# One test of a sum in place of two around the guarded slots, and the last kept slot's output moved behind it on GpSimd

## The chip, the core and the metric

The kernel runs on one core of a Trainium2 chip. Its engines are PE (TensorE, matmuls, with PEld for the loads of stationary operands), DVE (VectorE), ACT (ScalarE), POOL (GpSimd) and SP (SyncE, which here only issues transfers). Each engine has a sequencer that takes its own instructions in order and waits on semaphores; in the profile's rows an engine's name with a q behind it (POOLq, SPq) is that sequencer. The metric is the device time of one execution in microseconds (us).

## What is computed

A linear attention with random features gives `x`, and a mixture of experts is applied to each token of `x`:

```python
proj = np.einsum('bhsd,df->bhsf', x, w_phi)
proj = proj - np.max(np.abs(proj), axis=-1, keepdims=True)
phi = np.concatenate([np.exp(proj), np.exp(-proj)], axis=-1)   # for q and for k
kv = np.einsum('bhsf,bhsd->bhfd', k_p, v); z = np.sum(k_p, axis=2)
attn = einsum(q_p, kv) / (einsum(q_p, z) + 1e-6)               # -> x, (8, 576, 512)
...
logits = x @ w_gate                                            # 8 experts
fresh_e = argmax(logits); e = fresh_e if s == 0 or local_gate < 0.5 else prev_e
out[b, s] = softmax(logits)[e] * (np.maximum(x[b, s] @ w1[e], 0.0) @ w2[e])
```

There are 8 x 576 = 4608 tokens. Which expert a token goes to, and so how many tokens each expert gets, is known only on the device.

## The kernel before

The first half of the kernel computes the attention, 128 rows at a time, and the gate; each token's index and probability are scattered into a list by expert. The second half works through *slots*. A slot is one expert's weights with one, two or four groups of 128 tokens of that expert: quads (four groups), pairs (two) and singles (one), and *duals*, in which two half-filled groups of two experts share one group. A slot gathers its tokens by an indirect transfer from GpSimd (`gather_x`), transposes them, runs layer 1 (`layer1`) and layer 2 (`layer2`), scales the result by the probability into a tile `y` on DVE (line 948), and writes `y` to the rows of `out` by another indirect transfer from GpSimd (line 949). Weights arrive through SP as `wraw`, ACT casts them to a high part `whi` (line 797) and DVE forms the rest `wlo` (line 798); ACT and DVE do the same for the layer-1 result, `hh` (line 896) and `hl` (line 897).

`plan_main` (from line 662) counts, on DVE, how many slots of each kind the drawn tokens need. The lists are sized for the largest case. Ten singles are laid out and four duals; `moe` (line 988) always runs the first four singles and the first two duals, mixed among the quads and pairs, and the last of that order is a single. The six other singles and two other duals are *guarded*: each is in a branch that is entered only when the count says so, one nested in the other (`guarded`, line 982). The counts are two integers in memory, `left` (singles needed) and `halves` (half groups needed). Every engine loads `left` (line 999), compares and branches (line 984), then loads `halves` (line 1001) and branches again. With the data of this case no guarded slot is entered.

A tile that an engine writes or a transfer fills is guarded by semaphores that count. An engine that jumps over a guarded block therefore runs a short false path instead, in which it adds to its semaphores what the skipped instructions would have added. On GpSimd this is a wait for each of its eight transfer semaphores (DMASW0 to DMASW7) and then one INC_SWDGE_SEM, which adds to them. At the end every engine takes a DRAIN and meets the others at two barriers; SP first checks all the final semaphore values.

A scheduler orders the instructions of each engine by readiness and priority; on PE the order of the first half is written out by hand.

Of the kernel before, what the change touches and what calls it, by code (L numbers as in the profile page):

```python
# [6 lines left out]
F32 = mybir.dt.float32  # L7
F32R = mybir.dt.float32r
BF16 = mybir.dt.bfloat16
I32 = mybir.dt.int32  # L10
AF = mybir.ActivationFunctionType
ALU = mybir.AluOpType
# [5 lines left out]
DM, E, FF = 512, 8, 1024  # L18
# [3 lines left out]
NT = B * S  # L22
# [21 lines left out]
HALFWAY, EARLY, QUADS, PAIRS, SINGS, GUARD, DUALS, GUARD_D = 2, 3, 3, 7, 10, 6, 4, 2  # L44
# [4 lines left out]
class Kernel:  # L49
# [555 lines left out]
    def plan_early(self, bp):  # L605
# [39 lines left out]
        if bp == 1:  # L645
            yield from self.early_chores(slots, got())
        else:

            g = got()
            for x in g:  # L650
                if not self.scattering:
                    break
                yield x

            def last():
                for _ in g:
                    pass
                for s in slots:
                    self.gather_x(s)
            self.fetched_last = last  # L660

    def plan_main(self):
        dve = self.dve
        cq, size, half, mq, mp, ms, mps = (self.slotc[:, i:i + 1] for i in range(7))
        u1, u = self.units_so_far(127, 7, "m1"), self.units_so_far(63, 7, "m")
# [5 lines left out]
        ih = self.prefix(hf, "ih")  # L671
# [8 lines left out]
        for z in (0, 1):  # L680
            name = f"h{z}"
# [26 lines left out]
        i1 = self.prefix(f1, "i1")  # L708
        self.left = self.psm([1, 1], "left", I32)
        dve.tensor_copy(self.left, i1[0:1, E - 1:E])  # L710

        def mix(a, b, c, name):
            t = self.psm([NU, E], name)
            dve.tensor_scalar(t, a, mq, None, ALU.mult)
            dve.scalar_tensor_tensor(t, b, mp, t, ALU.mult, ALU.add)
            dve.scalar_tensor_tensor(t, c, ms, t, ALU.mult, ALU.add)
            return t

        incl = mix(i4, i2, i1, "im")
        cnt = mix(f4, f2, f1, "cm")  # L720

        bef = self.psm([NU, E], "bef")
# [11 lines left out]
        f = self.fetch(es, k, NU, "m", 1, rh)  # L734
        next(f)
        yield
        try:
            next(f)
        except StopIteration as r:
            tok, prob = r.value  # L740
        at = 0
# [183 lines left out]
            self.used(1)  # L925
        return [lambda: turn(2), lambda: turn(3)]

    def layer2(self, s, gi, between):
        tc, dve, pool = self.tc, self.dve, self.pool
        hh, hl = s["h"][gi]  # L930
        u0 = s["u"] + sum(s["n"][:gi])
        for k in range(s["n"][gi]):
            self.l2n = getattr(self, "l2n", 0) + 1
            p = self.psr if hasattr(self, "psr") and self.l2n % 3 else self.psm4
            t = p.tile([128, DM], F32, name="l2")
            o = slice(k * 128, k * 128 + 128)
            for f in range(8):
                c = slice((f % 2) * DM, (f % 2) * DM + DM)
                self.both(s, 4 + f // 2, t, hh[:, f, o], hl[:, f, o], c, f == 0, f == 7)
                if f in (0, 2) and between:  # L940
                    between.pop(0)()
                if f % 2 and gi == len(s["n"]) - 1 and k == s["n"][gi] - 1:
                    self.used(1)
                elif f % 2:
                    self.spare()
            y = self.mx2.tile([128, DM], F32, name="y")
            u = u0 + k
            dve.tensor_scalar_mul(y, t, s["prob"][:, u:u + 1])  # L948
            ins = pool.indirect_dma_start(  # L949
                self.A["out"], bass.IndirectOffsetOnAxis(s["tok"][:, u:u + 1], 0), y, None,  # L950
                bounds_check=NT - 1, oob_is_err=False)
            tc.declare_no_dep(ins.ins, group="outs", reason="each token is written once")
            tc.add_to_no_dep_group("outs", ins.ins)

    def slots(self, order, asides={}, final=None):
        first = order[0]
        for g in range(len(first["n"])):
            for f in self.tokens(first, g):
                f()
        self.held = len(first.get("w", ()))  # L960
        self.coming = list(order)
        for i, s in enumerate(order):
            while len(s.get("w", ())) < 8:
                self.spare()
            new = order[i + 1] if i + 1 < len(order) else None
            last = len(s["n"]) - 1
            for gi in range(last):
                self.layer1(s, gi, [])
            between = self.tokens(new, 0) if new else [lambda: None, final] if final else []
            rest = self.layer1(s, last, between)  # L970
            if i in asides:
                asides[i]()
            for f in between:
                f()
            for gi in range(last + 1):
                self.layer2(s, gi, rest)
            if new and len(new["n"]) == 2:
                for f in self.tokens(new, 1):
                    f()
            s.clear()  # L980

    def guarded(self, slots, count, i, per):
        if i < len(slots):
            with self.tc.If(count > per * i):
                self.slots([slots[i]])
                self.guarded(slots, count, i + 1, per)

    def moe(self):

        few = self.ss[:SINGS - GUARD]  # L990
        for i, x in enumerate(self.ds[:DUALS - GUARD_D]):
            few.insert(3 * i, x)
        rest = self.qs + self.ps_
        order = []
        per = len(rest) / len(few)
        for i, x in enumerate(few):
            order += rest[round(i * per):round((i + 1) * per)] + [x]
        self.slots(order)
        left = self.nc.values_load(self.left, min_val=0, max_val=63)  # L999
        self.guarded(self.ss, left, SINGS - GUARD, 1)  # L1000
        halves = self.nc.values_load(self.halves, min_val=0, max_val=63)
        self.guarded(self.ds, halves, DUALS - GUARD_D, 2)


def body(tc, A):
# [78 lines left out]
```

## Time and profile before

| | us |
|---|---|
| median of 3 runs (832.83 to 834.94) | 834.59 |
| the profiled execution | 827.76 |
| its span, first to last instruction | 825.9 |
| mean granted clock of PE in it | 0.982 of full |

The profiled execution's time stands 1.9 us above its span. A row of a group reads: line, engine, operation, output <- input, count, and durations or busy time. A row of the timeline reads: start, duration, engine, line, operation, tiles, and in brackets how long the engine had been idle before it and what ended that. The busy digits of the page, here PE and the DMA share in 40 equal slices of the span, show that PE is loaded nearly throughout and that the last slice and a half is empty:

```profile
PE   6999999999978899889999999999999999999980
DMA  6554556855898633473942775833966689867100
```

### The profile page before, as it was taken

How to read it: one execution, taken by the hardware profiler on the slowest of the kernel's cores; microseconds unless marked ns; L12 is line 12 of the kernel's file. 1: busy time of each engine (PE TensorE's matmuls, PEld its weight loads, DVE VectorE, ACT ScalarE, POOL GpSimd, SP SyncE). 2: the span in 40 equal slices, each digit the busy share in tenths (PEclk: the TensorE clock that was granted, in tenths of full speed). 3: DMA queues.
4: the chain of work that ended last, by engine and by line, in shares of the span. 5: the costliest groups of instructions: out<-in, count | busy, mean ns of one | idle time of the engine just before them, and what ended most of it. 6: DMA issues, size and time to landing. Idle time of an engine off the chain costs nothing. (4 is left out here: it accounts for less than half of the span.)

```text
span 825.9 us, 23190 instructions
## 1 busy us (share of the span) xinstructions
PE 772.5 (94%) x9674; PEld 681.2 (82%) x9674; DVE 519.9 (63%) x945; ACT 400.9 (49%) x708; POOL 138.9 (17%) x154
## 2 busy tenths in 40 slices
PE   6999999999978899889999999999999999999980
PEld 5899988888877888878888997698998996789970
DVE  5677898689778886748744224544856715776510
ACT  4666666566656565432632123533745515664410
POOL 0000002200230231242511202102222212011110
PEclk9999999999999999999999999999999999999995
DMA  6554556855898633473942775833966689867100
GB/s 194 140 134 129 145 130 117 129 137 132 151 216 226 177 77 85 107 182 106 388 166 90 264 281 205 270 115 111 356 220 211 219 312 409 303 238 238 53 28 15
DMA packets 74994, 148.71 MB, mean 180 GB/s; under 512 B 9044, under 2 KB 48610, under 8 KB 74864
## 3 DMA queue, kind: packets, MB, share of 16 engines
q1 hardware_dynamic: 67424, 127.33, 51.5%
q0 software_dynamic: 7392, 19.49, 7.0%
q8 instruction: 80, 1.31, 0.8%
q10 hardware_dynamic: 64, 0.30, 0.1%
q14 instruction: 34, 0.28, 0.1%
HBM read 128.18 MB, written 19.73 MB: 179 GB/s over the span
## 5 line engine op out<-in xcount | busy, mean ns | idle before, releaser
L797 ACT CAST whi<-wraw 128x1024 fp32r<-128x1024 f32 x136 | 142.2, 1048 | 154.5 <-PE l L865 67.1
L798 DVE TENSOR_TENSOR wlo<-wraw,whi 128x1024 fp32r<-128x1024 f32 x136 | 166.1, 1223 | 79.1 <-ACT whi L797 77.3
L863 PE MATMUL l<-xhi,whi 128*128 128x256 f32 x512 | 147.9, 289 | 3.5 <-DVE hl L897 2.8
L864 PE MATMUL l<-xlo,whi 128*128 128x256 f32 x512 | 145.5, 284 | 0.3 <-DVE xlo L859 0.3
L865 PE MATMUL l<-xhi,wlo 128*128 128x256 f32 x512 | 145.1, 283 | 0.0
L188 DVE TENSOR_REDUCE m<-pj 128x8 f32<-128x1024 f32 x72 | 87.8, 1219 | 46.4 <-PE pj L185 46.1
L863 PE MATMUL l<-whi,hh 128*128 128x512 f32 x288 | 114.2, 396 | 0.3 <-DVE y L948 0.3
L208 ACT ACTIVATE qp<-qt 128x512 f32<-128x512 f32 x144 | 84.6, 604 | 60.5 <-PE qt L205 58.2
L865 PE MATMUL l<-whi,hl 128*128 128x512 f32 x288 | 113.1, 393 | 0.0
L864 PE MATMUL l<-wlo,hh 128*128 128x512 f32 x288 | 112.8, 392 | 0.0
L194 ACT ACTIVATE kp<-sb 128x512 f32<-128x512 f32 x144 | 82.9, 623 | 53.2 <-DVE sb L190 44.3
L863 PEld LDWEIGHTS l<-xhi,whi 128*128 128x128 f32 x512 | 99.0, 194 | 6.2 <-DVE hl L897 3.4
L864 PEld LDWEIGHTS l<-xlo,whi 128*128 128x128 f32 x512 | 98.9, 193 | 1.0 <-DVE xlo L859 0.5
L865 PEld LDWEIGHTS l<-xhi,wlo 128*128 128x128 f32 x512 | 98.9, 193 | 0.1
L185 PE MATMUL pj<-first,kq 64*128 64x128 f32 x1152 | 87.2, 291 | 6.8 <-DMA kq<-in_kqT 6.4
L286 PE MATMUL nm<-kvs,qp 128*64 128x74 f32 x2304 | 87.0, 228 | 4.1 <-issue 3.1
L190 DVE TENSOR_TENSOR sb<-pj,m 128x1024 f32<-128x1024 f32 x72 | 88.1, 1223 | 3.6
L286 PEld LDWEIGHTS nm<-kvs,qp 128*64 128x64 f32 x2304 | 79.4, 136 | 5.1 <-issue 3.4
L185 PEld LDWEIGHTS pj<-first,kq 64*128 64x128 f32 x1152 | 72.7, 193 | 12.8 <-issue 5.9
L949 POOL DMA_INDIRECT out<-y,p_tokm x32 | 40.2, 1256 | 254.9 <-DVE y L948 254.3
L227 PE MATMUL kvp<-v,kp 128*64 128x65 f32 x2048 | 76.5, 224 | 0.3 <-issue 0.2
L896 ACT ACTIVATE hh<-l 128x512 fp32r<-128x512 f32 x64 | 38.1, 595 | 71.6 <-PE l L865 71.6
(229 smaller groups left out, 1037.6 us busy)
## 6 DMA issues: line engine op xcount, KB each, us to landing
wraw<-in_w1h SPq DMA_DIRECT2D x68, 512.0 KB, 5.9
wraw<-in_w2h SPq DMA_DIRECT2D x68, 512.0 KB, 6.3
kq<-in_kqT SPq DMA_DIRECT2D x47, 384.0 KB, 3.8
v<-in_va SPq DMA_DIRECT2D x48, 195.0 KB, 3.3
xs<-xo SPq DMA_DIRECT2D x48, 128.0 KB, 4.3
whi<-in_w1h SPq DMA_DIRECT2D x8, 512.0 KB, 4.2
wlo<-in_w1h SPq DMA_DIRECT2D x8, 512.0 KB
whi<-in_w2h SPq DMA_DIRECT2D x8, 512.0 KB, 7.2
```

What stands on the lines that cost most here:

```text
L185: self.last_pe = self.pe.matmul(t[:, h, i % 2, j, :], kq[r, j, s], self.w2[r], start=True, stop=True)
L188: dve.tensor_reduce(m, f, AX.X, ALU.max, apply_absolute_value=True)
L190: self.last_dve = dve.tensor_sub(sb.rearrange("p h c j f -> p (h c j) f"), f, m.unsqueeze(2).broadcast_to([128, 8, 128]))
L194: self.last_act = act.activation(kp[:, :, :, sg, :].rearrange("p c h f -> p h c f"), sb[:, :, :, 0], AF.Exp, scale=1.0 - 2 * sg)
L208: self.act.activation(qp[:, sg], t, AF.Exp, scale=1.0 - 2 * sg)
L227: self.pe.matmul(self.kvp[r, sg, h], self.ch[i]["kp"][:, h, sg, r], self.v(i, b)[:, h], start=first and n < 2, stop=last and n >= 6)
L286: self.pe.matmul(e["t"][r, c - c0, h, :], self.ch[i]["qp"][:, sg, h, q0 + r.start:q0 + r.stop], kvs[:, sg, h, :], start=sg == 0, stop=sg == 1)
L797: self.act.copy(hi, raw)
L798: self.dve.tensor_sub(lo, raw, hi.bitcast(F32))
L863: mm(o, ah, bh, start=first, stop=False)
L864: mm(o, ah, bl, start=False, stop=False)
L865: self.last_pe = mm(o, al, bh, start=False, stop=last)
```

## The change

`plan_main` gets three more operations on single numbers. They form `over` = max(left - 4, 0) + max(halves - 4, 0), which is above zero exactly when one of the two guarded lists would be entered. `moe` tests `over` once; the loads of `left` and `halves` and both nests of branches move inside that test. The last kept slot's output transfer isn't issued in `layer2` any more but handed back in a list (`held`) and issued after the test, from a tile `yl` of its own with one buffer.

```diff
+        over = self.psm([1, 2], "over")
+        dve.tensor_scalar(over[:, 0:1], i1[0:1, E - 1:E], float(GUARD - SINGS), 0.0, ALU.add, ALU.max)
+        dve.tensor_scalar(over[:, 1:2], ih[0:1, E - 1:E], float(2 * (GUARD_D - DUALS)), 0.0, ALU.add, ALU.max)
+        self.over = self.psm([1, 1], "overi", I32)
+        dve.tensor_add(self.over, over[:, 0:1], over[:, 1:2])
...
-    def layer2(self, s, gi, between):
+    def layer2(self, s, gi, between, held=None):
...
-            y = self.mx2.tile([128, DM], F32, name="y")
+            y = self.mx2.tile([128, DM], F32, name="yl", bufs=1) if held is not None else self.mx2.tile([128, DM], F32, name="y")
             u = u0 + k
             dve.tensor_scalar_mul(y, t, s["prob"][:, u:u + 1])
-            ins = pool.indirect_dma_start(
-                self.A["out"], bass.IndirectOffsetOnAxis(s["tok"][:, u:u + 1], 0), y, None,
-                bounds_check=NT - 1, oob_is_err=False)
-            tc.declare_no_dep(ins.ins, group="outs", reason="each token is written once")
-            tc.add_to_no_dep_group("outs", ins.ins)
+
+            def put(y=y, at=s["tok"][:, u:u + 1]):
+                ins = pool.indirect_dma_start(self.A["out"], bass.IndirectOffsetOnAxis(at, 0), y, None,
+                                              bounds_check=NT - 1, oob_is_err=False)
+                tc.declare_no_dep(ins.ins, group="outs", reason="each token is written once")
+                tc.add_to_no_dep_group("outs", ins.ins)
+            if held is None:
+                put()
+            else:
+                held.append(put)
...
-                self.layer2(s, gi, rest)
+                self.layer2(s, gi, rest, None if new else held)
...
-        self.slots(order)
-        left = self.nc.values_load(self.left, min_val=0, max_val=63)
-        self.guarded(self.ss, left, SINGS - GUARD, 1)
-        halves = self.nc.values_load(self.halves, min_val=0, max_val=63)
-        self.guarded(self.ds, halves, DUALS - GUARD_D, 2)
+
+        held = []
+        self.slots(order, held=held)
+        over = self.nc.values_load(self.over, min_val=0, max_val=63)
+        with self.tc.If(over > 0):
+            left = self.nc.values_load(self.left, min_val=0, max_val=63)
+            self.guarded(self.ss, left, SINGS - GUARD, 1)
+            halves = self.nc.values_load(self.halves, min_val=0, max_val=63)
+            self.guarded(self.ds, halves, DUALS - GUARD_D, 2)
+        for f in held:
+            f()
```

What this makes of the queues is seen in the built programs. The rows below show an instruction's line, name, tiles and the semaphores that it waits for. On GpSimd, at the end of the kept slots, before (the first row is the output before the last, the second the last one):

```order
L949 DMA out<-y,p_tokm 4608x512 [waits DMASW3_49,DVE_49]
L949 DMA out<-y,p_tokm 4608x512 [waits DMASW4_49,DVE_49]
L999 TENSOR_LOAD p_left [waits DVE_49]
L984 COMPARE_AND_BRANCH
L825 DMA xg<-xs,p_tokm 128x512 [waits DMASW5_49,PE_49]
```

And now, in the changed program's line numbers, up to the first guarded gather:

```order
L957 DMA out<-y,p_tokm 4608x512 [waits DMASW3_49,DVE_49]
L1012 TENSOR_LOAD p_overi [waits DVE_49]
L1013 COMPARE_AND_BRANCH
L1014 TENSOR_LOAD p_left
L995 COMPARE_AND_BRANCH
L831 DMA xg<-xs,p_tokm 128x512 [waits DMASW4_49,PE_49]
```

The test now follows the output before the last directly; the last output has gone from this place. It stands behind the false path of the test, near the end of GpSimd's program (ISA is here INC_SWDGE_SEM at line 1013, and the clearing of semaphores at line 1097):

```order
L995 ISA [waits DMASW6_49,DMASW7_49,DMASW5_49,DMASW4_49]
L995 UNCONDITIONAL_BRANCH
L1013 UNCONDITIONAL_BRANCH
L1013 ISA [waits Pool_sequencer_49,DMASW4_49,DMASW5_49,DMASW3_49,DMASW6_49,DMASW2_49,DMASW7_49,DMASW1_49,DMASW0_49]
L1013 UNCONDITIONAL_BRANCH
L957 DMA out<-yl,p_tokm 4608x512 [waits DMASW4_49,DVE_49]
L1097 UNCONDITIONAL_BRANCH
```

Before, two such false paths stood behind the last output, one for each test.

The scheduler also moves a few instructions at the start of the second half, around 385 to 422 us of the profile. On DVE, where the planning ends and the first slot's layer 1 begins, before:

```order
L562 TENSOR_SCALAR p_rim<-p_rowm 36x1
L948 TENSOR_SCALAR y<-l_6672,p_probe 128x512
L897 SCALAR_TENSOR_TENSOR hl<-l_6704,hh 128x512
L798 TENSOR_TENSOR wlo<-wraw,whi 128x1024 x2
L897 SCALAR_TENSOR_TENSOR hl<-l_6731,hh 128x512
```

And now:

```order
L562 TENSOR_SCALAR p_rim<-p_rowm 36x1
L954 TENSOR_SCALAR y<-l_6677,p_probe 128x512
L804 TENSOR_TENSOR wlo<-wraw,whi 128x1024
L903 SCALAR_TENSOR_TENSOR hl<-l_6709,hh 128x512
L804 TENSOR_TENSOR wlo<-wraw,whi 128x1024
L903 SCALAR_TENSOR_TENSOR hl<-l_6736,hh 128x512
```

The first tile's `hl` has moved behind one weight difference `wlo`; on ACT its `hh` has moved behind the cast of that weight in the same way. Some 25 us later on DVE, before:

```order
L798 TENSOR_TENSOR wlo<-wraw,whi 128x1024 [waits DMAHW3_49,Activation_49]
L948 TENSOR_SCALAR y<-l_6849,p_probf 128x512 [waits DMASW2_49,PE_49]
L798 TENSOR_TENSOR wlo<-wraw,whi 128x1024 [waits DMAHW4_49,Activation_49]
L859 TENSOR_TENSOR xlo<-tr,xhi 128x4x128 [waits Activation_49] x2
L798 TENSOR_TENSOR wlo<-wraw,whi 128x1024 [waits DMAHW0_49]
```

And now:

```order
L804 TENSOR_TENSOR wlo<-wraw,whi 128x1024 [waits DMAHW3_49,Activation_49]
L804 TENSOR_TENSOR wlo<-wraw,whi 128x1024 [waits DMAHW4_49,Activation_49]
L954 TENSOR_SCALAR y<-l_6854,p_probf 128x512 [waits DMASW2_49,PE_49]
L865 TENSOR_TENSOR xlo<-tr,xhi 128x4x128 [waits Activation_49] x2
L804 TENSOR_TENSOR wlo<-wraw,whi 128x1024 [waits DMAHW0_49]
```

That slot's `y` has moved behind one more `wlo`, and on GpSimd one output of that stretch has changed places with a gather. On SP the load of `halves` is gone from this stretch, and the load of `left` has become one of `over`. From there to the last slot the order on each engine is as before.

More of the change, by code (lines that the diff above doesn't have):

```diff
@@ L945, in layer2, with slots @@
                     self.spare()
-            y = self.mx2.tile([128, DM], F32, name="y")
+            y = self.mx2.tile([128, DM], F32, name="yl", bufs=1) if held is not None else self.mx2.tile([128, DM], F32, name="y")
             u = u0 + k
             dve.tensor_scalar_mul(y, t, s["prob"][:, u:u + 1])
-            ins = pool.indirect_dma_start(
-                self.A["out"], bass.IndirectOffsetOnAxis(s["tok"][:, u:u + 1], 0), y, None,
-                bounds_check=NT - 1, oob_is_err=False)
-            tc.declare_no_dep(ins.ins, group="outs", reason="each token is written once")
-            tc.add_to_no_dep_group("outs", ins.ins)
-    def slots(self, order, asides={}, final=None):
+            def put(y=y, at=s["tok"][:, u:u + 1]):
[7 more added lines that the diff above has]
+                held.append(put)
+    def slots(self, order, asides={}, final=None, held=None):
         first = order[0]
```

## The prediction

> **What bounds the kernel now.** I read the page first, then the stretches of the last 26 us, then the sequencer instructions of single lines there, and last the stretch around 380 to 427 us, where the order of work changes.
>
> ```profile
> span 825.9 us, 23190 instructions
> PE 772.5 (94%) x9674; PEld 681.2 (82%) x9674; DVE 519.9 (63%) x945; ACT 400.9 (49%) x708; POOL 138.9 (17%) x154
> POOL out L949 0%; POOLq L999 0%
> 600.00:803.00 203.00, 202.97 (x1306) 175.20 (x1304) 116.05 (x131) 94.83 (x133) 32.69 (x25) 1.00 0.63 226
> 800.00:804.00 4.00, 2.97 (x13) 2.06 (x11) 1.11 (x2) 0.00 (x0) 0.00 (x0) 1.00 0.03 6
> 804.00:806.00 2.00, 0.00 (x0) 0.00 (x0) 0.00 (x0) 0.00 (x0) 0.98 (x1) 0.93 0.28 90
> ```
>
> The columns of a stretch are start and end, length, busy time of PE, PEld, DVE, ACT and POOL, granted clock, DMA share and GB/s. PE is the bound up to 803 us (202.97 of 203.00). Then nothing that counts as busy happens but one POOL instruction, and the span goes on to 825.9. The chain that ended last is no help: its two entries, both 0%, stop at that instruction. The tail is made of sequencer work that no busy share shows, so I read it line by line.
>
> ```profile
> 803.00 0.75 DVE L948 TENSOR_SCALAR y<-l,p_probm 128x512 f32<-128x512 f32 x1 [2.64 <-PE l L865]
> L949 POOL DMA_INDIRECT out<-y,p_tokm x1: 983/983/983, 804.0 to 804.0; - x1
> DMA to landing us min/median/max: 5.3/5.3/5.3
> L999 POOLq TENSOR_LOAD <-p_left x1: 502/502/502, 803.8 to 803.8; - x1
> L984 POOLq EVENT_SEMAPHORE  x6: 17/43/43, 809.3 to 812.8; - x6
> L984 POOLq INC_SWDGE_SEM  x2: 2511/2520/2528, 809.7 to 812.9; - x2
> L1080 POOLq DRAIN  x3: 46/107/9617, 815.5 to 825.6; - x3
> L1080 SPq EVENT_SEMAPHORE  x14: 17/28/28, 812.1 to 825.9; - x14
> ```
>
> Each row gives count, shortest/median/longest in ns, and the first and last start. They add up to one chain on GpSimd. The last `y` is ready at 803.75; its output is issued from 804.03 to 805.02 and lands at 804.0 + 5.3 = 809.3. The branch on `left` is not taken into the guarded slots, and the path around them first waits for every GpSimd queue, the output just issued included: its first semaphore row starts at 809.3, the landing. Then one INC_SWDGE_SEM of 2.5 us (it credits the DMAs that the skipped slots would have counted), the load of `halves`, a second one from 812.9 to 815.4, and the DRAIN from 815.46 for 9.62 us to 825.08. Closing barriers take the remaining 825.9 - 825.1 = 0.8. So **the tail after the issue is 20.9 us: 4.3 to the landing, 6.1 of credits and tests, 9.6 of DRAIN, 0.8 of barriers.**
>
> **The change, part by part.**
>
> *The output behind the test.* The order shows the test of `over` on GpSimd straight behind the output before the last, and the last output (`yl`) behind the false path of that test. The credit now waits for the output before the last.
>
> ```profile
> L949 POOL DMA_INDIRECT out<-y,p_tokm x1: 983/983/983, 791.9 to 791.9; - x1
> DMA to landing us min/median/max: 2.7/6.2/8.5
> L984 POOLq COMPARE_BRANCH  x2: 45/50/54, 804.4 to 812.6; - x2
> ```
>
> It is issued at 791.9 and lands between 2.7 and 8.5 us later, at 794.6 to 800.4. Load and branch (0.5 + 0.05) lie inside that. Semaphores take 809.7 - 809.3 = 0.4, the credit 2.5: done at 797.5 to 803.3. `yl` is ready at 803.75, so even the longest landing leaves 0.4 us. Cover: PE's last slot. If it were gone, what is late is the output, us for us. The landing of 5.3 and one credit of 2.5 with its checks thus leave the path, and the second credit, its load and checks exist no more.
>
> *What is late next.* Behind `yl` stands only the branch to the end and DRAIN. With the issue over at 805.02, DRAIN starts there instead of at 815.46: **10.44 us earlier**, if it still takes 9.6. Does it? That is the unknown that matters.
>
> ```profile
> L1074 POOLq DRAIN  x1: 188/188/188, 0.3 to 0.3; - x1
> L1074 POOLq INC_SWDGE_SEM  x1: 31/31/31, 0.1 to 0.1; - x1
> lst<-pr,ri POOLq DMA_INDIRECT x36, 7.4
> xg<-xs,p_tokm POOLq DMA_INDIRECT x32, 6.7
> out<-y,p_tokm POOLq DMA_INDIRECT x32, 6.2
> ```
>
> At the start, with no GpSimd DMA behind it, DRAIN takes 0.19 us and INC_SWDGE_SEM 0.03. At the end, with these 100 and 17 smaller ones behind, 9.62 and 2.5, and the two DRAINs that follow take 0.11 and 0.05. Nothing was in flight from 809.3 on, so the long one was not waiting for data. That reads as work per earlier DMA, some 9617/117 = 82 ns each (my estimate), done once. The number of DMAs is unchanged, so I take 9.6; bounds are 0.1 (the next DRAIN) and 9.6 counted from the landing at 809.3. The walk outlasts the landing, so that one is hidden.
>
> The Trainium skill ("VectorE: DVE Perf Modes", section "The DRAIN you can't avoid") says that the closing DRAINs on all five engines are boilerplate of a constant 12 ns or so. The trace disagrees for GpSimd (9617 ns); by that sentence the long one would be a wait for something else, and the sum would come out as in the rival of the short DRAIN below.
>
> *One test in place of two, other engines.*
>
> ```profile
> L984 PEldq COMPARE_BRANCH  x2: 3847/4312/4776, 801.0 to 805.6; - x2
> L1080 PEldq DRAIN  x2: 8/8/8, 810.5 to 825.4; - x2
> ```
>
> PE loses one taken branch of 4 to 5 us and reaches its end near 806 instead of 810.5; SP's fourteen checks go from the landing on, 0.7 us of them. Both finish before 815, so both are worth nothing.
>
> *Three tiny DVE operations and a moved order, at 383 to 422 us.*
>
> ```profile
> 387.36 0.14 DVE L710 CAST p_left<-p_i 1x1 int32<-1x1 f32 x1
> 387.43 0.20 DVE L716 SCALAR_TENSOR_TENSOR p_im<-p_i,consts,p_im 36x8 f32<-36x8 f32 x1
> 392.35 0.60 ACT L896 ACTIVATE hh<-l 128x512 fp32r<-128x512 f32 x1 [12.40 <-PE l L865]
> 393.39 1.05 ACT L797 CAST whi<-wraw 128x1024 fp32r<-128x1024 f32 x1 [0.44 <-DMA wraw<-in_w1h]
> 392.98 0.69 DVE L897 SCALAR_TENSOR_TENSOR hl<-l,hh 128x512 fp32r<-128x512 f32 x1 [1.38 <-ACT hh L896]
> 394.47 1.23 DVE L798 TENSOR_TENSOR wlo<-wraw,whi 128x1024 fp32r<-128x1024 f32 x1 [0.80 <-ACT whi L797]
> 395.32 0.38 PE L863 MATMUL l<-xhi,whi 128*128 128x256 f32 x1
> 398.79 0.38 PE L863 MATMUL l<-xhi,whi 128*128 128x256 f32 x1 [0.46 <-DVE hl L897]
> 416.71 0.74 DVE L948 TENSOR_SCALAR y<-l,p_probf 128x512 f32<-128x512 f32 x1
> 421.89 1.28 DVE L897 SCALAR_TENSOR_TENSOR hl<-l,hh 128x512 fp32r<-128x512 f32 x2
> 422.62 0.38 PE L863 MATMUL l<-xhi,whi 128*128 128x256 f32 x1 [1.87 <-DVE hl L897]
> ```
>
> A 1x1 operation holds DVE 0.07 us (387.36 to 387.43), three of them 0.2. Dearer is the order: `hh` and `hl` of the first layer-1 tile now stand behind a weight's cast and difference. `hl` then ends near 394.47 + 1.23 + 0.69 = 396.4 instead of 393.7. PE's third tile, which takes over that buffer, started at 395.32, so it waits some 1.1 us; the 0.46 wait at 398.79 takes part of it back. Later a `y` (0.74) now stands behind one more difference, on a DVE that is busy from 418 to 423, and moves the `hl` that PE awaits at 422.62 by about 0.4. That wait of 1.87 also swallows what was lost before. I take **0.5 us lost**, between a gain of 0.5 (the wait at 398.79 gone) and a loss of 2.2 (one more drop of the clock, priced below). PE is full from there on, so this reaches the end. SP's dropped load of `halves` gains nothing: its next loads wait for later results of the same DVE chain.
>
> **Sum.** 10.44 - 0.5 = 9.9 us off the profiled 827.76 (span 825.9 and 1.9 around it): 817.8. The median of the runs shown is 834.59, 6.8 above the profiled run; I carry that over unchanged: **834.59 - 9.9 = 824.7**. About 0.3%, 2.5 us, is what a measurement of this kernel can tell from no change.
>
> **Rivals.**
> - *DRAIN is short* (its 9.6 us belong to the two late credits, which now run beside PE). For it: both stand right ahead of it. Against it: SP's checks are let go at 812.1, when the first credit ends, so a credit is complete by then. The end is then the landing: 809.3 + 0.7 + 0.8 + 0.5 = 811.3, 14.6 less: 820.0.
> - *DRAIN starts counting at the landing*: 809.3 + 9.6 + 0.8 + 0.5 = 820.2, 5.7 less: 828.9. Against it: before, it began 6 us after the landing and showed no such wait.
> - *The change does nothing for the end*: DRAIN ends a fixed 20.1 us after the last issue (825.1 - 805.0), whatever stands between. Then only the 0.5 counts: 835.1. Only one such DRAIN is in the trace, so it can't be excluded, but nothing else in the trace runs on such an interval.
> - *Slower*: the moved `hh`. It now waits for a weight's transfer, which in this run landed in time (393.39).
>
> ```profile
> wraw<-in_w1h SPq DMA_DIRECT2D x68, 512.0 KB, 5.9
> 423.00:424.00 1.00, 1.00 (x9) 1.00 (x8) 0.17 (x1) 0.00 (x0) 0.00 (x0) 0.72 0.01 4
> 424.00:425.00 1.00, 1.00 (x7) 1.00 (x6) 0.00 (x0) 0.00 (x0) 0.00 (x0) 0.50 0.00 0
> 425.00:426.00 1.00, 1.00 (x7) 1.00 (x6) 0.00 (x0) 0.00 (x0) 0.00 (x0) 0.50 0.00 0
> 426.00:427.00 1.00, 1.00 (x7) 1.00 (x7) 0.00 (x0) 0.00 (x0) 0.00 (x0) 0.57 0.00 0
> ```
>
> Each us that it lands later holds PE for one, and a wait like that of 1.87 was followed by these four rows with clocks of 0.72, 0.50, 0.50 and 0.57: together 0.28 + 0.50 + 0.50 + 0.43 = 1.7 us. It decides from 10.4 - 1.7 = 8.7 us of lateness on, more than the 5.9 that such a transfer takes; at 12 us late the time is 834.6 + 12 + 1.7 - 10.4 = 837.9. Unlikely.
>
> **How the numbers follow.** Forecast 0.72 (own range 823 to 827), short DRAIN 0.12, from the landing 0.07, nothing gained 0.06, slower 0.03. The range takes the first two and their middle terms: 819.5 to 827.3, leaving out 0.16. Faster by over 0.3%: 0.72 + 0.12 + 0.07 = 0.91; within it 0.06; slower 0.03.
>
> **What would show it.** In the profile after: one INC_SWDGE_SEM, ended before 803.3, and none behind the last output; the issue of `yl` still at 804 to 805; one DRAIN record that starts near 804 and ends near 815 (some 10.6 long, the issue in it); PE's share after 427 us unchanged and some 0.5 us later. I am wrong if DRAIN's end doesn't move, if `yl` is issued later than its `y` allows, or if PE's waits between 392 and 423 grow by more than 2 us.

## The result, and the profile after

Measured beside each other, the changed kernel took 823.93 us (median of 4, 820.66 to 828.31) and the kernel before 833.71 (median of 4): a ratio of 0.9886 with a 95% interval of 0.9836 to 0.9935, or 9.5 us less (4.1 to 4.2 us to either side). Ratios here and below leave out executions that took over 1.5% longer than the fastest of their kernel, the profiled one of the kernel before once more (839.69 us) among them. The profiled execution took 824.28 us, its span is 822.5, the granted clock 0.987.

The end of the program first. These are GpSimd's rows from 790 us on, by line of the changed kernel (L1012 loads `over`, L1013 is the test and its false path, L957 the output, L1097 the end), with count, shortest/median/longest in ns and the first and last start:

```profile
L1012 POOLq TENSOR_LOAD <-p_overi x1: 494/494/494, 798.7 to 798.7; - x1
L957 POOL DMA_INDIRECT out<-y,p_tokm x2: 984/984/984, 793.4 to 799.0; - x2
L1013 POOLq EVENT_SEMAPHORE  x5: 17/43/2011, 799.8 to 802.1; - x5
L1013 POOLq INC_SWDGE_SEM  x1: 2508/2508/2508, 802.2 to 802.2; - x1
L957 POOL DMA_INDIRECT out<-yl,p_tokm x1: 984/984/984, 811.0 to 811.0; - x1
L1097 POOLq DRAIN  x3: 46/113/10843, 810.8 to 822.2; - x3
L1097 SPq EVENT_SEMAPHORE  x14: 17/28/28, 814.9 to 822.5; - x14
```

The output before the last is issued at 799.0; GpSimd waits 2.0 us for its landing (the longest semaphore row), credits once from 802.2 to 804.7 and is then idle for six microseconds, until `yl` is ready. Behind the last issue (811.05 to 812.03) stands nothing but the DRAIN. Its record begins at 810.81, before the issue that it contains, and ends 10.84 us later at 821.66, so 9.62 us after the issue. SP's checks, which the landing lets go, begin at 814.9, so the landing doesn't set the DRAIN's end, 6.8 us later. **From the start of the last issue to the end of the span it is 822.5 - 811.05 = 11.45 us, where it was 825.9 - 804.03 = 21.87: 10.4 us less.**

PE has lost one taken branch and reaches its end at 812, ten microseconds before the DRAIN is over:

```profile
L1013 PEldq COMPARE_BRANCH  x1: 3555/3555/3555, 808.1 to 808.1; - x1
L1097 PEldq DRAIN  x2: 8/8/8, 812.0 to 822.1; - x2
```

But the spans differ by 3.4 us only, since the last `y` is ready 7 us later in this profile than in that of before. Three rows of DVE's timeline (start, duration, engine, line, operation) cut the way to it: the count `left`, the first `y` of a main slot, and the last:

```profile
392.81 0.13 DVE L710 CAST p_left<-p_i 1x1 int32<-1x1 f32 x1
451.46 0.75 DVE L954 TENSOR_SCALAR y<-l,p_probm 128x512 f32<-128x512 f32 x1 [4.25 <-PE l L871]
810.02 0.75 DVE L954 TENSOR_SCALAR yl<-l,p_probm 128x512 f32<-128x512 f32 x1 [2.60 <-PE l L871]
```

And in the kernel before the second of them (the other two were shown: 387.36 and 803.00):

```profile
447.35 0.75 DVE L948 TENSOR_SCALAR y<-l,p_probm 128x512 f32<-128x512 f32 x1 [4.17 <-PE l L865]
```

Up to `left` the profile after is 392.81 - 387.36 = 5.4 us late, in the half of the kernel where both programs do the same. From there to the first main `y` it takes 58.65 us in place of 59.99, and from that to the last **358.56 in place of 355.65, 2.9 us more, with the clock at 1.00 and PE full in both**. The first of these three is put down to the execution: in another execution of the kernel before (below) `left` came at 401.50 us, and half-speed stretches of the clock fell at other places in these two. The windows below (start and end, length, busy time of PE, PEld, DVE, ACT, POOL, clock, DMA share, GB/s) show 145 to 149 us, first after, then before:

```profile
145.00:149.00 4.00, 3.06 (x54) 2.99 (x54) 0.63 (x3) 2.27 (x6) 0.00 (x0) 0.57 0.66 192
```

```profile
145.00:149.00 4.00, 4.00 (x100) 3.63 (x96) 3.26 (x7) 1.97 (x5) 1.16 (x2) 1.00 1.00 96
```

The last of the three, 2.9 us in a stretch whose instructions and order are the same, was not foreseen. What it is, and whether the 9.6 us of DRAIN are what the prediction took them for, are the questions of the experiments.

### The profile page after: what moved, and what is told of

Its sections match the earlier page's. It is cut to its first block, busy times and chain, and to the rows that moved or that the text cites. A ratio compares the mean times of both kernels' runs of the same rounds, so it can differ in the third digit from the quotient of the medians.

```text
span 822.5 us, 23169 instructions
## 1 busy us (share of the span) xinstructions
PE 778.1 (95%) x9674; PEld 685.4 (83%) x9674; DVE 520.2 (63%) x948; ACT 400.4 (49%) x708; POOL 140.8 (17%) x154
## 4 chain that ended last, share of the span: by engine, by line
PE 62%; issue 17%; DMA 7%; DVE 7%; POOL 3%; ACT 2%; another core or an unknown queue 1%; SPq 1%; POOLq 0%; DVEq 0%; ACTq 0%
PE l L869 10%; PE l L870 9%; PE l L871 9%; PE kvp L227 8%; PE pj L185 8%; PE nm L286 8%; DMA out<-y,p_tokm 4%; PE qt L205 4%; PE l L882 2%; POOL out L957 2%; DVE sb L190 2%; DVE m L188 1%; PE tr L855 1%; PE nm L265 1%; POOL xg L831 1%
## 5 line engine op out<-in xcount | busy, mean ns | idle before, releaser
L286 PE MATMUL nm<-kvs,qp 128*64 128x74 f32 x2304 | 89.6, 230 | 9.2 <-ACT kvs L267 5.0
L286 PEld LDWEIGHTS nm<-kvs,qp 128*64 128x64 f32 x2304 | 81.5, 139 | 10.6 <-ACT kvs L267 5.5
L957 POOL DMA_INDIRECT out<-y,p_tokm x31 | 39.2, 1265 | 245.8 <-DVE y L954 245.2
L227 PEld LDWEIGHTS kvp<-v,kp 128*64 128x64 f32 x2048 | 67.5, 139 | 6.4 <-issue 5.4
```

The costliest lines, as they stand in the source:

```text
L227: self.pe.matmul(self.kvp[r, sg, h], self.ch[i]["kp"][:, h, sg, r], self.v(i, b)[:, h], start=first and n < 2, stop=last and n >= 6)
L286: self.pe.matmul(e["t"][r, c - c0, h, :], self.ch[i]["qp"][:, sg, h, q0 + r.start:q0 + r.stop], kvs[:, sg, h, :], start=sg == 0, stop=sg == 1)
```

## The experiments

Three measures run through them. The *tail* is the time from the start of the last output's issue to the end of the span. The *main stretch* is the time between the starts of the first and the last main `y`. The *middle* is the time from the cast of `left` to the first main `y`. The expectations count the main stretch from a matmul near 438 us, where the change lost 3.2 to 3.3 us in place of the 2.9 between the two rows of `y`; the difference lies ahead of the first `y`.

### The kernel before, once more

> The kernel before, unchanged: it shows how much two executions of one program differ. In the two profiles shown so far the last output's issue started at 804.03 (before) and at 811.05 (after), 7.0 us later, most of it gathered where both programs are alike. Theory (chance: clock drops that fall at other places, and a spread that is not the change's): this profile's last output starts more than 1 us away from 804.03, and the ratio's interval holds 1. Rival (the 7.0 us belong to the changed program): it starts within 1 us of 804.03. Either way the time from the start of the last issue to the end of the span is again 21.9 us, and the closing DRAIN of GpSimd 9.6 us.

The ratio is 0.9992 (0.9955 to 1.0028). Of the profiled execution only stretches are used: the last output started at 816.96, 12.9 us later than in the first profile of the same program, the tail was 837.9 - 816.96 = 20.9 us (the landing took 4.3 us, not 5.3), the closing DRAIN 9617 ns to the nanosecond, the main stretch 355.77. What the execution decides is therefore the way up to the first main `y`, and by several microseconds; that `y` started at 460.2 us here and at 443.8 to 455.6 us in the other profiles, while the main stretch repeats within tenths.

### One part alone: the output held, two tests

```diff
-        over = self.psm([1, 2], "over")
...
-        dve.tensor_add(self.over, over[:, 0:1], over[:, 1:2])
...
-        over = self.nc.values_load(self.over, min_val=0, max_val=63)
-        with self.tc.If(over > 0):
-            left = self.nc.values_load(self.left, min_val=0, max_val=63)
...
+        left = self.nc.values_load(self.left, min_val=0, max_val=63)
+        self.guarded(self.ss, left, SINGS - GUARD, 1)
+        halves = self.nc.values_load(self.halves, min_val=0, max_val=63)
+        self.guarded(self.ds, halves, DUALS - GUARD_D, 2)
         for f in held:
             f()
```

> One part alone: the last output held behind the false paths, but with the two tests of before and without the three operations that form the sum. The order at 383 to 422 us is that of before. My theory (both credits hide beside the matmuls of the last slot): the output before the last lands some 3 to 6 us after its issue, and two credits with load and checks take 6.1 us from there, done 9 to 12 us after that issue; y comes 11.8 us after it. So the last output is not late by more than a few tenths, and from the start of its issue to the end of the span it is 11.4 us as in the profile after (822.5 - 811.05); time against before 10.4 us less, ratio 0.9875. Rival 1 (the saving needs the single test): the second credit and its load stand on the path, 14.5 us from the issue or the issue 3 us behind its y, ratio 0.991. Rival 2 (the moved hh and hl cost 0.5 us or more): this one is faster than the change by that.

Ratio 0.9936 (0.9902 to 0.9969). GpSimd's rows:

```profile
L951 POOL DMA_INDIRECT out<-yl,p_tokm x1: 985/985/985, 808.9 to 808.9; - x1
L989 POOLq INC_SWDGE_SEM  x2: 2508/2510/2511, 800.4 to 809.3; - x2
L1089 POOLq DRAIN  x3: 46/107/9617, 811.9 to 822.1; - x3
```

The tail is 822.4 - 808.87 = 13.5 us, 2.1 more than in the change. My expectation that both credits stand ahead of the output was wrong: the scheduler put the output between the two tests, so the first credit (800.4) hides beside PE's last slot and the second (809.3 to 811.9) comes behind the issue. It doesn't wait for the last output to land, though, and neither does the start of the DRAIN: it begins at 811.9, 2.0 us behind the issue and 2.9 before SP's checks of the landing (814.8), and takes the same 9617 ns. That speaks against a DRAIN counted from the landing, and against one that ends a fixed time after the last issue (20.1 us before, 9.6 after, 11.7 here). The main stretch is 356.18 us, with `yl` in its place: 0.5 more than before, not 2.9.

### The other part alone: one test, the output at its old place

```diff
-        held = []
-        self.slots(order, held=held)
+        self.slots(order)
...
-        for f in held:
-            f()
```

> The other part alone: one test of the sum, the last output at its old place ahead of it. The moved hh, hl and y at 383 to 422 us are those of the change. My theory (the tail is landing, then credits, then DRAIN, one after the other): the second credit with its load and checks (815.4 - 812.2 = 3.2 us) is gone and the rest stays, so 21.9 - 3.2 = 18.7 us from the start of the last issue to the end of the span; with 0.5 us lost in the middle the time is 2.7 us less than before, ratio 0.9968. Rival 1 (DRAIN ends a fixed 20.1 us after the last issue): 21.9, ratio 1.0006. Rival 2 (DRAIN counts from the landing): 5.3 + 9.6 + 0.8 = 15.7 us, ratio 0.993. If the tile yl were the reason why the profile after was 3.4 us slower between 430 and 803 us, this kernel, which has no yl, would not show that.

Ratio 1.0024 (0.9986 to 1.0062): no gain, where 0.9968 was expected. GpSimd's rows:

```profile
L1012 POOLq INC_SWDGE_SEM  x1: 2528/2528/2528, 813.4 to 813.4; - x1
L1094 POOLq DRAIN  x3: 46/107/9617, 816.0 to 826.2; - x3
```

The tail is 826.5 - 808.45 = 18.05 us, 3.8 less than before (3.2 for the second credit and its load, and a landing of 4.65 in place of 5.3). So one test alone is worth 3.2 us, as worked out, and the rest of the 10.4 is the landing and the other credit that the held output moves off the path. The main stretch is 358.56, 2.9 us longer than before, without any `yl`, so the tile `yl` isn't its cause; and it takes nearly all of the gain away.

### An early DRAIN

```diff
                 tc.add_to_no_dep_group("outs", ins.ins)
+                if self.l2n == 35:
+                    with tc.issue_after(ins.ins):
+                        pool.drain()
```

> The change with one more DRAIN on GpSimd, behind the fourth-last kept output, while PE still has some 40 us of matmuls. Theory (the DRAIN is work per DMA issued since the last one, about 82 ns each): the early one takes about 9 us beside PE, and the closing one only waits for the last output's landing and works off four more DMAs; 5.3 to 7 us from the start of the issue, 0.4 us of work and 0.8 us of barriers give 6.5 to 8.2 us from the start of the last issue to the end of the span, in place of 11.4: 3 to 5 us less than the change, ratio to before 0.983. The credit (INC_SWDGE_SEM) may get shorter too; that costs and gains nothing there. Rival 1 (the closing DRAIN takes 9.6 us whatever came before, or ends a fixed time after the last issue): it stays 11.4 us, no gain, ratio 0.988. Rival 2 (the early DRAIN holds up the outputs or gathers behind it): PE waits in the last 50 us, where it has no wait now.

Ratio 0.9867 (0.9825 to 0.991). The early DRAIN, the credit and the closing DRAIN:

```profile
L963 POOLq DRAIN  x1: 11330/11330/11330, 780.5 to 780.5; - x1
L1016 POOLq INC_SWDGE_SEM  x1: 235/235/235, 806.4 to 806.4; - x1
L1100 POOLq DRAIN  x3: 46/113/4008, 814.9 to 820.1; - x3
```

The early one takes 11.33 us with the issue of 1.72 and 0.23 ahead of it, so 9.38 behind that issue, beside a full PE. Ahead of it stand 114 of the kernel's 117 transfers and three behind it, not 113 and four as the expectations here and in the next section count. The credit is now 0.24 us, and the closing DRAIN's record 4.0, of which 2.8 lie behind the issue. It ends at 818.9, just as SP's checks of the landing begin (818.8); these and the barriers follow. The tail is 820.4 - 815.15 = 5.25 us, below the 6.5 to 8.2 expected because the output landed in under 4 us. **So the 9.6 us are not a fixed time: they are work left over from earlier transfers, which can be done earlier, beside PE's work.** Outputs behind the early DRAIN were not late, and the main stretch is the change's, 358.56.

### Forty and eight more GpSimd transfers

```diff
+            more = self.const.tile([1, 640], F32, name="more")
+            for k in range(40):
+                self.pool.dma_start(more[:, 16 * k:16 * k + 16], A["zrow"][:, 0:16])
```

> The change with 40 more GpSimd transfers of 64 bytes each at the start of the program (what they write is not used). What is known of the closing DRAIN: 9.617 us after 117 GpSimd transfers, 9.38 us for the early one of the last experiment after 113 (11.33 less the 1.72 and 0.23 ahead of it), and 2.8 us for its closing one after 4 more. Through these goes a line of 2.6 us and 60 ns per transfer, not the 82 ns of my prediction; the INC_SWDGE_SEM of 2.51 and of 0.235 us gives some 20 ns per transfer. Theory (work per earlier transfer): DRAIN takes 9.6 + 40 x 0.06 = 12.0 us (12.9 at 82 ns), INC_SWDGE_SEM 3.3 us, and the span is 2.4 us longer behind the last issue (13.9 in place of 11.45). Rival 1 (a fixed time): 9.6 and 2.5 as before. Rival 2 (work per row or byte moved; the 40 move one row each against up to 128 of the others): 9.6 to 9.7.

The closing DRAIN and the credit became shorter, not longer:

```profile
L1016 POOLq INC_SWDGE_SEM  x1: 886/886/886, 804.2 to 804.2; - x1
L1100 POOLq DRAIN  x3: 46/115/6420, 813.0 to 820.3; - x3
```

The record of 6.42 us leaves 5.2 behind the issue, 4.4 less than without the forty. Both the theory and its rivals missed. One of GpSimd's issues stands out in the trace: the 129th of the 157 began 1.9 us after its `y` was ready, where the same output takes 0.3 in the change. The next run was made to see whether the work had been done there. It is the same kernel with `range(8)`:

> As with the forty more transfers, but eight, 125 in all. With forty more (157 in all) the closing DRAIN did not grow to 12 us but shrank to 5.2 us behind the issue, and INC_SWDGE_SEM from 2.51 to 0.89; the 129th transfer was issued 1.9 us after its y was ready (0.28 in the change). Theory (the work is per transfer since the last clearing, and a clearing happened by itself at the 129th): with 125 none happens, so DRAIN grows: 9.617 us after 117 and 9.38 after 113 make 59 ns each, so 9.617 + 8 x 0.059 = 10.1 us behind the issue, and INC_SWDGE_SEM 2.51 + 8 x 0.02 = 2.7 us. Rival 1 (early small transfers shorten the DRAIN in some other way): it shrinks here too, by a fifth of the 4.4 us, to 8.7. Rival 2 (9.6 is a ceiling): 9.6 and 2.5.

```profile
L1016 POOLq INC_SWDGE_SEM  x1: 360/360/360, 807.5 to 807.5; - x1
L1100 POOLq DRAIN  x3: 46/115/4944, 814.5 to 820.4; - x3
```

Here, too, theory and rivals missed: with 125 transfers the DRAIN is shorter still (4.94, 3.7 behind the issue). The timeline points at a reason (the `y` of the output before the last on DVE, then two issues on GpSimd):

```profile
801.57 0.75 DVE L957 TENSOR_SCALAR y<-l,p_probm 128x512 f32<-128x512 f32 x1 [4.82 <-PE l L874]
797.03 0.98 POOL L960 DMA_INDIRECT out<-y,p_tokm  x1 [15.05 <-DVE y L957]
804.19 0.99 POOL L960 DMA_INDIRECT out<-y,p_tokm  x1 [6.17 <-issue]
```

The second issue, the 124th transfer, began 1.9 us after its `y` (801.57 + 0.75 = 802.32), and its wait is put down to no engine. So in both kernels one issue held GpSimd for some 1.6 us longer than usual, and the credit behind it was short. That fits a store of some 120 transfers that is cleared when it is full, which the 117 of the kernel don't reach; no run shows the clearing itself. At some 20 ns per transfer the credits of 0.36 and 0.886 us stand for about 8 and 35 transfers (my estimate from 0.235 us for the two of the early DRAIN's kernel), seven more than were issued from the stalled one on, so not everything was cleared there. What is counted (transfers, rows or bytes: eight small ones brought the clearing to the 124th, forty to the 129th) is open. Part of the 5.2 and 3.7 us is the wait for the landing: SP's checks begin at 818.0 and 819.0, and the DRAIN ends 1.5 and 0.4 us later. Why the 29 transfers from the stalled one on leave 1.5 us behind the landing, when 29 x 82 ns = 2.4 us would fit into the 3.7 ahead of it, is open too.

The Trainium skill gives a size for such a store: "SBUF — State Buffer" (section "SBUF size: 192, 224, or 256?") sets 16 KiB of each partition aside for the rings into which GpSimd writes its descriptors, and "DMA: Bandwidth & Descriptors" (sections "Terms" and "The descriptor swizzle") has 16 bytes for a descriptor and 9 of them per engine and direction for a transfer of 1 MiB to 128 partitions. My estimate from these pages, with one partition to a ring, is 16384 / 16 / 9 = 113 such transfers. That is near the 120 or so seen here, but the kernel's own 117, of at most 256 KB each, show no such stall. No run shows a ring itself.

### 64 bytes

The kernels with the sum have two more small tiles in SBUF, which moved the tiles allocated behind them by 64 bytes: in the built programs nine of the thirteen buffers of `whi` and of `wlo`, all of `wraw` and `xg`, and one of the two of `hh` and `hl`. They moved together in all the experiments, so which of them counts was not tested. The edit moves them by 64 more, in the change and in the kernel before, with the same instructions in the same order:

```diff
-        self.left = self.psm([1, 1], "left", I32)
+        self.left = self.psm([1, 24], "left", I32)[:, 0:1]
```

> The change with 64 bytes more per partition of unused SBUF among the planner's small tiles: the same instructions in the same order, and every tile allocated behind (whi, wlo, hh, hl among them) stands 64 bytes further. Three kernels with the sum's two tiles, which moved those by 64 bytes against before (whi from byte 26912 to 26976), ran the matmuls from 438 us on to the end slower: 3.2 to 3.3 us over the stretch, 256-column matmuls 119 to 120 ns apart in place of 117 to 118; the two without the sum did not (0.3 and 0.7 us), whether or not they had the tile yl. Theory (the address of the tiles that PE reads, by its place within 128 bytes: 32 before, 96 in the change): at 27040 it is 32 again, the stretch is back within 0.5 us of before and the time 3 us below the change, ratio to before 0.985. Rival 1 (the moved instructions, or three more on DVE): the stretch stays 3.2 us longer, ratio 0.988. Rival 2 (a larger power of two): the stretch takes some other value.

> The kernel before with the same 64 bytes of unused SBUF, so that whi, wlo, hh and hl stand where the change has them, and nothing else: the same instructions in the same order. Theory (address): the matmuls from 438 us to the last take 3.2 us longer than before, and the time is 3.2 us above it, ratio 1.004. Rival 1 (order or instructions): no difference in that stretch, ratio 1.000.

The second of them decides. The first and the last main `y` of the kernel before with 64 bytes more:

```profile
443.82 0.75 DVE L948 TENSOR_SCALAR y<-l,p_probm 128x512 f32<-128x512 f32 x1 [4.25 <-PE l L865]
802.36 0.75 DVE L948 TENSOR_SCALAR y<-l,p_probm 128x512 f32<-128x512 f32 x1 [2.59 <-PE l L865]
```

That makes 358.54 us, where the change has 358.56 and before 355.65, and the ratio is 1.0053 (1.002 to 1.0086). **Moving the tiles by 64 bytes costs 2.9 us, without any other part of the change.** In the change, 64 bytes further gave 805.51 - 447.86 = 357.65, so 0.9 were regained and not all of it; the place within 128 bytes, my theory, is not the rule. The ratio there is 0.992 (0.9887 to 0.9953).

The groups of PE between 460 and 790 us (line, tiles, shapes, count, busy us, mean ns of one) show where the time goes. Before, and then with 64 bytes:

```profile
L863 PE MATMUL l<-xhi,whi 128*128 128x256 f32 x352 | 100.4, 285 | 0.0
L865 PE MATMUL l<-xhi,wlo 128*128 128x256 f32 x352 | 98.7, 280 | 0.0
L864 PE MATMUL l<-xlo,whi 128*128 128x256 f32 x352 | 98.7, 280 | 0.0
L863 PE MATMUL l<-whi,hh 128*128 128x512 f32 x204 | 80.6, 395 | 0.0
L865 PE MATMUL l<-whi,hl 128*128 128x512 f32 x205 | 80.5, 393 | 0.0
L864 PE MATMUL l<-wlo,hh 128*128 128x512 f32 x205 | 80.2, 391 | 0.0
```

```profile
L863 PE MATMUL l<-xhi,whi 128*128 128x256 f32 x352 | 100.9, 287 | 0.0
L865 PE MATMUL l<-xhi,wlo 128*128 128x256 f32 x352 | 99.5, 283 | 0.0
L864 PE MATMUL l<-xlo,whi 128*128 128x256 f32 x352 | 99.4, 282 | 0.0
L863 PE MATMUL l<-whi,hh 128*128 128x512 f32 x200 | 79.1, 396 | 0.0
L865 PE MATMUL l<-whi,hl 128*128 128x512 f32 x201 | 79.1, 394 | 0.0
L864 PE MATMUL l<-wlo,hh 128*128 128x512 f32 x201 | 79.1, 393 | 0.0
```

By their busy time the 1056 matmuls of 256 columns take 0.5 + 0.8 + 0.7 = 2.0 us more. Those of 512 columns take 1 to 2 ns more each, some 200 x (1 + 1 + 2) = 0.8 us (an estimate from rounded means). So both kinds are slower, and together they make up 2.8 us of the 2.9.

### Early DRAIN with other places of the tiles

> Early DRAIN and 64 bytes together. The early DRAIN took the time from the start of the last issue to the end of the span down to 5.25 us (expected 6.5 to 8.2), 6.2 us less than the change; with whi back at 32 within 128 bytes the stretch from 438 us on gains 3.2 us by the address theory. Together 21.9 - 5.25 = 16.6 us below before, ratio 0.980. By rival 1 of the two experiments above the 3.2 us stay: 13.4 us below, ratio 0.984.

> As with early DRAIN and 64 bytes, but 32 bytes further than the change: whi, wlo and one hh and hl start on a multiple of 128 (27008). The stretch from 438 us to the last matmul took, against before: at 26912 0.3 to 0.7 us more, at 26976 3.2 to 3.3, at 27040 2.3, at 29536 (26976 + 5 x 512) 3.2. Theory (the place within 512 bytes or a smaller power of two decides): a value between 0 and 3.3, different from that of 26976. Rival 1 (a multiple of 64 is better than any place at 32 beyond one): below 0, faster than before. The time: 4.9 to 6.4 us from the last issue to the end, so ratio 0.980 at 0, 0.984 at 3.3.

> The change with the early DRAIN, and the sum's numbers kept in the padding of the tile of the count left, so that whi, wlo and one hh and hl stand at the addresses of before. Theory (address): the stretch from 438 us to the last matmul takes 0.3 to 0.7 us more than in the profile before, where the change took 3.2 and 128 bytes further 2.3; with 5.3 to 6.4 us from the start of the last issue to the end of the span the time is 15 to 16.5 us below before, ratio 0.981. Rival (the three more operations and the moved order make the matmuls slower, not the address): 3.2 in that stretch, ratio 0.984.

The first two take `[1, 24]` and `[1, 16]` for the tile of `left`, with the early DRAIN. The third keeps all numbers of the sum in the padding of that tile, so that nothing moves but `yl`'s neighbours at the other end of SBUF:

```diff
-        self.left = self.psm([1, 1], "left", I32)
+        four = self.psm([1, 4], "left", I32)
+        self.left, over, self.over = four[:, 0:1], four[:, 1:3], four[:, 3:4]
...
-        over = self.psm([1, 2], "over")
...
-        self.over = self.psm([1, 1], "overi", I32)
```

The ratios are 0.9826 (0.978 to 0.9873), 0.9854 (0.9801 to 0.9907) and 0.9809 (0.9748 to 0.987). The main stretch of the third:

```profile
447.05 0.75 DVE L953 TENSOR_SCALAR y<-l,p_probm 128x512 f32<-128x512 f32 x1 [4.17 <-PE l L870]
802.72 0.75 DVE L953 TENSOR_SCALAR yl<-l,p_probm 128x512 f32<-128x512 f32 x1 [2.64 <-PE l L870]
```

It takes 355.67 us, the 355.65 of before, with the sum, its three operations and the moved order all in. By the first byte of `whi`, all profiles:

| `whi` at byte | place within 512 | main stretch, us | kernels |
|---|---|---|---|
| 26912 | 288 | 355.40 to 356.18 | before, the same again, two tests held, early DRAIN in before, sum in the padding |
| 26976, 29536 | 352 | 358.53 to 358.56 | the change, one test alone, early DRAIN, 64 bytes in before; forty and eight more |
| 27008 | 384 | 359.57 | early DRAIN and 32 bytes |
| 27040 | 416 | 357.65 | 64 bytes in the change, early DRAIN and 64 bytes |

A start on a multiple of 128 (27008) is the slowest, so a start on such a multiple is no help. Why the place counts is not settled. The Trainium skill ("SBUF — State Buffer", section "Who interferes with whom") lets only the port pair shared by GpSimd and VectorE cause contention, PE sharing with nobody. By that the stretch would be the same at each place; the runs show 355.4 to 359.6. They don't show that it is contention.

### The early DRAIN in the kernel before

The same three lines as above behind the output of `layer2`, and nothing else of the change.

> The kernel before with nothing but the early DRAIN behind the fourth-last kept output: two tests, last output ahead of them, all tiles at the addresses of before. Theory (credits and DRAIN are short once an early DRAIN has cleared the earlier transfers): from the start of the last issue to the end of the span 4.7 to 5.3 us to the landing, two credits of 0.24 with load, branch and checks 1.2, DRAIN 0.2 to 0.4, barriers 0.8, so 6.9 to 7.7 in place of 21.9: 14.5 us less, ratio 0.983. The change's own two parts would then be worth only about 1.5 us more on top. Rival (the closing DRAIN after late credits keeps a floor of 2.6 us, from the line through 113 and 4 transfers): 9.5 us, ratio 0.985.

Ratio 0.9841 (0.9789 to 0.9893), against 0.983 expected.

```profile
L949 POOL DMA_INDIRECT out<-y,p_tokm x1: 984/984/984, 805.6 to 805.6; - x1
L987 POOLq INC_SWDGE_SEM  x2: 231/240/248, 809.8 to 810.7; - x2
L1083 POOLq DRAIN  x3: 46/107/294, 811.0 to 812.2; - x3
```

Landing, two credits of 0.24 us, a DRAIN of 0.29: the tail is 812.5 - 805.60 = 6.9 us, 15 less than before. The floor of 2.6 us that I had drawn through what I took for 113 and 4 transfers was the wait for a landing; here the output has landed by then and 0.29 remain. **So, over the 114 transfers that the early DRAIN took off, DRAIN's time is (9617 - 294) / 114 = 82 ns per transfer that it finds, and the credit's (2528 - 248) / 114 = 20 ns.** These are means over transfers of several sizes (the 36 of `lst` move 128 rows of 8 bytes, most of the others 128 rows of 2 KB); whether the work goes by transfers, rows or bytes isn't shown.

### The sums

Tail and main stretch, from one profile of each kernel, agree with the measured ratios. For each kernel, both against before, their sum, and what was measured against the kernel before of the same series:

| kernel | tail, us | main stretch | sum against before | measured, 95% |
|---|---|---|---|---|
| before | 21.9 | 355.65 | | |
| the change | 11.45 | +2.9 | -7.5 | -9.5 (-13.7 to -5.4) |
| held, two tests | 13.5 | +0.5 | -7.8 | -5.3 (-8.2 to -2.6) |
| one test, not held | 18.05 | +2.9 | -0.9 | +2.0 (-1.2 to +5.2) |
| early DRAIN | 5.25 | +2.9 | -13.7 | -11.1 (-14.6 to -7.5) |
| 64 bytes in the change | 11.5 | +2.0 | -8.4 | -6.6 (-9.3 to -3.9) |
| 64 bytes in before | 22.4 | +2.9 | +3.4 | +4.4 (+1.7 to +7.1) |
| early DRAIN, 64 bytes | 6.4 | +2.0 | -13.5 | -14.4 (-18.2 to -10.5) |
| early DRAIN, 32 bytes | 6.4 | +3.9 | -11.5 | -12.2 (-16.6 to -7.8) |
| early DRAIN in before | 6.9 | -0.25 | -15.2 | -13.3 (-17.6 to -8.9) |
| early DRAIN, sum in the padding | 6.45 | 0.0 | -15.4 | -16.0 (-21.1 to -10.9) |

Each measured interval holds its sum, but the intervals are 5 to 10 us wide. The last row is the best by both columns; its interval overlaps those of the other early DRAINs.

## Why the prediction was right, and where it wasn't

- **The tail: right, term for term.** Forecast 10.44 us less, measured 10.4 (21.87 to 11.45). The tenths are luck: with other landings the tail before was 20.9 us (once more) and 22.4 (with 64 bytes). The DRAIN began with the issue, not with the landing, and took 9.62 us behind it. The credit had six microseconds to spare; the 0.4 that I had counted as the least was for a landing of 8.5 us.
- **DRAIN as work that earlier DMAs leave, 82 ns each: right.** That was the estimate from one DRAIN on which 9.6 us hung; the early DRAIN in the kernel before gives 82, too. What it left out is that the work isn't always left to the end: with 125 and 157 transfers the closing DRAIN was shorter, behind one issue that stalled.
- **The rivals.** A short DRAIN fell with the first profile. One counted from the landing fell with it too (SP's checks from 814.9, end at 821.66, 6.8 us on), and in the kernel with two tests. "Ends 20.1 us after the last issue" was 9.6 and 11.7. No late weight transfer showed: the one new wait of PE behind the moved `hh` is 0.6 us.
- **The middle, forecast 0.5 us lost: neither seen nor ruled out.** The moved `hl` held PE as said, but less. PE's waits from 380 to 450 us, after and then before:

```profile
PE l L869 <- DVE hl L903: 1.5, 2, 0.9
```

```profile
PE l L863 <- DVE hl L897: 2.3, 2, 1.9
```

  The new wait was 0.6 us (1.1 forecast), and the one at 422 fell from 1.9 to 0.9. The middle took 58.4 to 60.0 us in five profiles with the old order (mean 59.1) and 58.6 to 60.0 in nine with the new (mean 59.1). But the 60.0 of before holds the clock drop from 423 to 427 us that the prediction prices at 1.7 us, and in no other profile does the granted clock fall there. Without it the old order's mean would be 58.8, and the new order's loss some 0.3 us (an estimate). The profiles of one order differ by more than that.
- **"PE's share after 427 us unchanged": right for the share, wrong for the time.** PE was full in both, but 2.9 us longer over the same work. The step that failed is the one that priced the three operations at 0.2 us of DVE and a moved order: it took their two tiles as free, and they moved `whi`, `wlo` and others by 64 bytes.
- **The number.** 824.7 was forecast and 823.93 measured, 9.9 and 9.5 us less. By the measured parts the sum should have been 10.4 - 2.9 = 7.5. The interval of the measurement (5.4 to 13.7) holds both, so that the total came this close is luck in part. The 64 bytes in the kernel before and the sum in the padding show that the missing term is there. The 2.5 us that the prediction took for what a measurement can tell were 4.1 to 4.2 here.

## What to carry to other kernels

A long DRAIN at the end of a kernel with many GpSimd transfers is work that they left, 82 ns each here: one more DRAIN a little ahead of the end, under work of another engine, was worth more (15 us of tail) than all the reordering of the change (10.4). Where a kernel is bound by PE, even a tile of one number can have a price if it moves the tiles behind it: compare the same stretch of matmuls before and after, not only waits and order. And where one execution differs from the next by several microseconds, as here ahead of the main slots, read a change off stretches that repeat within tenths, then add them up.

## What the runs showed of the hardware that was not expected

- Where the tiles behind the planner's numbers (weights, gathered tokens, one `hh` and `hl`) start within SBUF changes the pace of the same matmuls: by the first byte of `whi`, the main stretch took 355.7 us at 26912, 358.5 at 26976, 359.6 at 27008, 357.7 at 27040, and the same 358.5 again five times 512 bytes further.
- More GpSimd transfers made the end shorter: eight transfers of 64 bytes at the start cut the closing DRAIN's record from 10.84 to 4.94 us and the credit from 2.51 to 0.36, after one issue that began 1.9 us behind its `y` in place of 0.3, beside a full PE.
